# Second layer of a two-layer MoE kernel: the down product in seven products for eight per pair of token tiles, up products in blocks of 256 columns

## The chip, the cores and the metric

The kernel runs on one core of a Trainium2 chip. The metric is the device time of one execution in microseconds (us), taken as the median of several runs; lower is better. Durations come from one profiled execution of the kernel before, whose own time stands in the table below. PE is TensorE, DVE VectorE, ACT ScalarE, POOL GpSimd, SP SyncE.

## What is computed

A gated linear attention gives 3072 tokens of 384 columns. A router sends each to one of 8 experts, and a second, dense layer follows; its last three lines are the ones that matter here:

```python
h = np.maximum(x[mask] @ w1[e], 0.0)          # expert e, 384 -> 1024
out[mask] = gate_w[mask, None] * (h @ w2[e])  # 1024 -> 384
...
h = x @ w_in                                  # every token, 384 -> 2048
g = np.maximum(0.01 * h, h)
return (g @ w_out).astype(np.float32)         # 2048 -> 384
```

Every fp32 operand of a product is held as a pair of fp16 tiles, a high part and the rest (`hi`, `lo`), and every product is three matmuls: hi by hi, lo by hi, hi by lo.

## The kernel before

All is one function, `body`. Attention and routing come first and write each token with its gate into a DRAM table by expert (`bucket`) with indirect DMAs of POOL. Then the experts run one after the other with 432 places each, and in front of expert 0 stands a part of its tokens, 256 columns wide (`early=True`), that does not wait for the table. An expert's up product (L976 to L978) goes through four PSUM banks `ps1`; a bank is emptied by ACT (L983, the high part) and DVE (L984, the rest). Its down product (L1002 to L1004) ends in `x2h`/`x2l` (L1013, L1014), the second layer's input, 3072 columns in expert order. Beside it the next expert's weights and the second layer's weights are fetched by SP (L927), converted on ACT and DVE (L932, L933; L949 to L955) and split into pairs. The order of this stage is written by a planner (`Plan`): every step has an engine, a duration, what it reads and writes and a due time, and the planner's list sets the program order of every engine. Each engine works its list strictly from the top.

The second layer (functions `second_in` and `second_out`) takes 512 columns at a time, six blocks. `second_in` makes 16 hidden slices `f` of 128 rows, nine matmuls of 512 columns each (L809 to L811). For every slice ACT takes 0.01 times the sum (L814), DVE the larger of the two (L815), ACT the high part (L817), DVE the rest (L818). Then `second_out` takes the block's four tiles of 128 tokens one by one: 16 slices of three matmuls of 384 columns (L826 to L828), scaled by the gate on ACT (L830) and scattered to the output by POOL (L831). 24 tiles make 24 times 48 of these matmuls; the up part is 6 times 16 times 9 = 864 matmuls. Some 30 small DVE steps (`past_static`, L1073 to L1110) work out which tokens lie past an expert's 432 places; none do in this data, so the loop behind them runs no time.

Of the kernel before, what the change touches and what calls it, by code (L numbers as in the profile page):

```python
# [21 lines left out]
P = 128  # L22
# [138 lines left out]
OVB = 32  # L161
E0 = 2 * P
# [9 lines left out]
def body(ctx, tc, qT, kT, aT, v, emb, tau, w1, w2, w_in, w_out, out):  # L172
# [4 lines left out]
    wps = [ctx.enter_context(tc.tile_pool(name="wp0", bufs=1))]  # L177
# [29 lines left out]
    hid = [[keep.tile([P, BLK], F16, name=f"h{x}{f}") for f in range(NF1)] for x in "hl"]  # L207
# [3 lines left out]
    def stage():  # L211
        return wst.tile([P, CH], F32, name="wstage")
# [18 lines left out]
    def expert_tiles():  # L231
        wps.append(wps.pop(0))
        return [wps[-1].tile([P, KD * F1], F16, name=n) for n in ("w1h", "w1l", "w2h", "w2l")]
# [43 lines left out]
    with tc.tile_pool(name="at", bufs=1) as rt, \  # L277
# [394 lines left out]
        w_first = expert_tiles()  # L672
# [86 lines left out]
    wps.insert(0, ctx.enter_context(tc.tile_pool(name="wp1", bufs=1)))  # L759
    big = ctx.enter_context(tc.tile_pool(name="big", bufs=1))  # L760
    x2h = big.tile([P, KD, X2], F16, name="x2h")
    x2l = big.tile([P, KD, X2], F16, name="x2l")
# [3 lines left out]
    wol = big.tile([P, NF2, D], F16, name="wol")  # L766

# [35 lines left out]
    def second_in(gp, gs, pp, xh, xl, n):  # L803
        ghs, gls = [], []
        for f in range(NF2):
            ps = pp.tile([P, n], F32, name="ps3")
            fs = slice(f * P, (f + 1) * P)
            for k in range(KD):
                nc.tensor.matmul(ps, wih[:, k, fs], xh[:, k], start=k == 0, stop=False)  # L809
                nc.tensor.matmul(ps, wih[:, k, fs], xl[:, k], start=False, stop=False)  # L810
                nc.tensor.matmul(ps, wil[:, k, fs], xh[:, k], start=False, stop=k == KD - 1)  # L811
            r = gs.tile([P, n], F32, name="r")
            g = gs.tile([P, n], F32, name="g")
            nc.scalar.activation(r, ps, AF.Copy, scale=0.01 * 2.0 ** -6)  # L814
            nc.vector.scalar_tensor_tensor(g, ps, 2.0 ** -6, r, op0=ALU.mult, op1=ALU.max)  # L815
            gh, gl = (hid[i][f][:, :n] if f < NF1 else gp.tile([P, n], F16, name=f"g{i}{f}") for i in range(2))
            nc.scalar.activation(gh, g, AF.Copy)  # L817
            nc.vector.tensor_tensor(gl, g, gh, op=ALU.subtract)  # L818
            ghs.append(gh)
            gls.append(gl)  # L820
        return ghs, gls

    def second_out(gs, pp, ghs, gls, ts, scale, index, dst):
        ps = pp.tile([P, D], F32, name="ps4")
        for f in range(NF2):
            nc.tensor.matmul(ps, ghs[f][:, ts], woh[:, f], start=f == 0, stop=False)  # L826
            nc.tensor.matmul(ps, ghs[f][:, ts], wol[:, f], start=False, stop=False)  # L827
            nc.tensor.matmul(ps, gls[f][:, ts], woh[:, f], start=False, stop=f == NF2 - 1)  # L828
        osb = gs.tile([P, D], F32, name="osb")
        nc.scalar.activation(osb, ps, AF.Copy, scale=scale)  # L830
        nc.gpsimd.indirect_dma_start(out=dst, out_offset=bass.IndirectOffsetOnAxis(ap=index, axis=0),  # L831
                                     in_=osb, in_offset=None, bounds_check=NT - 1, oob_is_err=False)

    with tc.tile_pool(name="mx", bufs=1) as mxp, \
# [3 lines left out]
        first = [stage() for _ in range(4)]  # L838
        sets = [w_first, expert_tiles()]
# [155 lines left out]
        def down(e, d, at, cols, early=False):  # L995
# [16 lines left out]
            where = [] if e == 0 else [("place", i) for i in range(2)]  # L1012
# [4 lines left out]
        with tc.manual_schedule():  # L1017
# [23 lines left out]
            for e in range(E):  # L1041
# [13 lines left out]
                for d in range(KD):  # L1055
                    down(e, d, begin(e) + 13.2 + 4.4 * d - 12.0, cols)
            for i in plan.order():
                plan.ops[i][2]()
# [125 lines left out]
```

## Time and profile before

| | |
|---|---|
| runs of the kernel before | 773.33 to 776.7 us, median 773.78 us of 3 |
| the profiled execution | 771.36 us, its span 769.7 us |
| TensorE busy | 745.8 us, 97% of the span |
| VectorE busy | 453.6 us, 59% |
| ScalarE busy | 342.2 us, 44% |
| GpSimd busy | 97.7 us, 13% |

A matmul's duration in the trace holds its way through the array, and matmuls overlap; what one costs in a stream is the distance from its start to the next one's start. An engine's idle time costs only where another waits for it. All times in the rows are microseconds from the start of the span, unless marked ns.

### The profile page before, as it was taken

The numbers are of one execution on the slowest core, as the hardware profiler recorded it, in microseconds if no ns is written. First come the engines' busy times: TensorE is split into PE (matmuls) and PEld (weight loads), VectorE is DVE, ScalarE is ACT, GpSimd is POOL, SyncE is SP. The second block draws the span as 40 slices with busy tenths as digits, with TensorE's granted clock in tenths as the row PEclk, the third lists the DMA queues.
The fourth block names the chain that finished last, engine by engine and source line by source line (L and its number), as shares of the span: only waits on it lengthen the run. The fifth ranks groups of instructions, "written<-read, shape, count | busy, mean of one in ns | idle before, by whom it ended". The sixth has DMA issues, their size and how long they took to land.

```text
span 769.7 us, 13141 instructions
## 1 busy us (share of the span) xinstructions
PE 745.8 (97%) x5190; PEld 432.1 (56%) x5190; DVE 453.6 (59%) x795; ACT 342.2 (44%) x686; POOL 97.7 (13%) x108
## 2 busy tenths in 40 slices
PE   7999999989999999999899999999999999999995
PEld 4777767658655555555444654654554564564462
DVE  8989899958786898888955036016206305503600
ACT  2344545537665777776544035025215305403500
POOL 6121615140001000000000100110010010010011
PEclk9999999999999999999999999999999999999998
DMA  8994945248998999866200000000000000000000
GB/s 284 347 302 123 280 144 195 68 151 208 221 219 183 230 259 223 251 188 206 44 1 0 21 21 1 21 22 0 11 32 1 10 21 11 1 25 18 0 22 23
DMA packets 58754, 84.48 MB, mean 110 GB/s; under 512 B 26680, under 2 KB 37952, under 8 KB 58688
## 3 DMA queue, kind: packets, MB, share of 16 engines
q1 hardware_dynamic: 55072, 74.06, 35.6%
q0 software_dynamic: 3616, 9.53, 3.3%
q8 instruction: 43, 0.70, 0.4%
q14 instruction: 23, 0.19, 0.1%
HBM read 66.80 MB, written 12.12 MB: 103 GB/s over the span
## 4 chain that ended last, share of the span: by engine, by line
issue 47%; PE 34%; DVE 6%; DMA 5%; POOL 3%; ACT 2%; SPq 1%; POOLq 0%; ACTq 0%; DVEq 0%
PE ps L977 4%; PE ps L976 4%; PE ps L978 4%; PE ps L1004 3%; PE ps L1003 3%; PE ps L1002 3%; POOL out L831 3%; PE psc L403 3%; PE py L454 2%; PE py L422 2%; DMA wstage<-in_w_in 2%; PE pfill L343 2%; DMA v<-in_v 1%; DMA wstage<-in_w 1%; PE ptr L482 1%
## 5 line engine op out<-in xcount | busy, mean ns | idle before, releaser
L815 DVE SCALAR_TENSOR_TENSOR g<-ps,r 128x512 f32<-128x512 f32 x96 | 65.8, 685 | 154.9 <-ACT r L814 154.9
L809 PE MATMUL ps<-x2h,wih 128*128 128x512 f16 x288 | 109.9, 382 | 2.7 <-DVE x2l L1014 2.7
L810 PE MATMUL ps<-x2l,wih 128*128 128x512 f16 x288 | 109.9, 382 | 0.0
L811 PE MATMUL ps<-x2h,wil 128*128 128x512 f16 x288 | 109.7, 381 | 0.0
L830 ACT ACTIVATE osb<-ps,ms 128x384 f32<-128x384 f32 x24 | 13.9, 581 | 160.9 <-PE ps L828 160.9
L1004 PE MATMUL ps<-hh,w2l 128*128 128x432 f16 (+2 forms) x216 | 70.2, 326 | 0.3 <-DVE w2l L933 0.2
L1002 PE MATMUL ps<-hh,w2h 128*128 128x432 f16 (+2 forms) x216 | 70.2, 326 | 0.0
L1003 PE MATMUL ps<-hl,w2h 128*128 128x432 f16 (+2 forms) x216 | 70.2, 326 | 0.0
L831 POOL DMA_INDIRECT out<-osb,tki x24 | 23.3, 973 | 359.7 <-ACT osb L830 352.9
L976 PE MATMUL ps<-xt,w1h 128*128 128x432 f16 (+1 forms) x192 | 63.6, 333 | 0.9 <-ACT xt L901 0.9
L977 PE MATMUL ps<-xt,w1h 128*128 128x432 f16 (+1 forms) x192 | 63.6, 333 | 0.5 <-DVE xt L902 0.5
L978 PE MATMUL ps<-xt,w1l 128*128 128x432 f16 (+1 forms) x192 | 63.6, 333 | 0.1
L828 PE MATMUL ps<-woh,hl 128*128 128x384 f16 x192 | 62.6, 326 | 0.0
L826 PE MATMUL ps<-woh,hh 128*128 128x384 f16 x192 | 62.6, 326 | 0.0
L827 PE MATMUL ps<-wol,hh 128*128 128x384 f16 x192 | 62.6, 326 | 0.0
L828 PE MATMUL ps<-woh,g 128*128 128x384 f16 x192 | 62.6, 326 | 0.0
L827 PE MATMUL ps<-wol,g 128*128 128x384 f16 x192 | 62.6, 326 | 0.0
L826 PE MATMUL ps<-woh,g 128*128 128x384 f16 x192 | 62.6, 326 | 0.0
L814 ACT ACTIVATE r<-ps 128x512 f32<-128x512 f32 x96 | 56.0, 583 | 12.5 <-PE ps L811 12.5
L818 DVE TENSOR_TENSOR hl<-g,hh 128x512 f16<-128x512 f32 x48 | 33.3, 693 | 33.4 <-ACT hh L817 33.4
L818 DVE TENSOR_TENSOR g<-g,g 128x512 f16<-128x512 f32 x48 | 33.2, 693 | 33.4 <-ACT g L817 33.4
L810 PEld LDWEIGHTS <-wih 128*128 128x128 f16 x288 | 28.3, 98 | 36.8 <-issue 3.5
(226 smaller groups left out, 1347.0 us busy)
## 6 DMA issues: line engine op xcount, KB each, us to landing
wstage<-in_w SPq DMA_DIRECT2D x64, 384.0 KB, 5.5
a<-in_aT SPq DMA_DIRECT2D x16, 387.5 KB, 4.9
k<-in_kT SPq DMA_DIRECT2D x16, 384.0 KB, 5.9
q<-in_qT SPq DMA_DIRECT2D x16, 384.0 KB, 6.6
wstage<-in_w_in SPq DMA_DIRECT2D x16, 384.0 KB, 6.9
wstage<-in_w_out SPq DMA_DIRECT2D x16, 384.0 KB, 3.5
v<-in_v SPq DMA_DIRECT2D x8, 576.0 KB, 9.5
xg<-bucket SPq DMA_DIRECT2D x6, 582.0 KB, 6.9
```

Source lines behind the costliest of these rows:

```text
L809: nc.tensor.matmul(ps, wih[:, k, fs], xh[:, k], start=k == 0, stop=False)
L810: nc.tensor.matmul(ps, wih[:, k, fs], xl[:, k], start=False, stop=False)
L811: nc.tensor.matmul(ps, wil[:, k, fs], xh[:, k], start=False, stop=k == KD - 1)
L826: nc.tensor.matmul(ps, ghs[f][:, ts], woh[:, f], start=f == 0, stop=False)
L827: nc.tensor.matmul(ps, ghs[f][:, ts], wol[:, f], start=False, stop=False)
L828: nc.tensor.matmul(ps, gls[f][:, ts], woh[:, f], start=False, stop=f == NF2 - 1)
L976: nc.tensor.matmul(ps, w1h[:, f, k], xt[:, k], start=k == 0, stop=False)
L977: nc.tensor.matmul(ps, w1h[:, f, k], xt[:, KD + k], start=False, stop=False)
L978: nc.tensor.matmul(ps, w1l[:, f, k], xt[:, k], start=False, stop=k == KD - 1)
L1002: nc.tensor.matmul(ps, w2h[:, f, ds_], hh, start=f == 0, stop=False)
L1003: nc.tensor.matmul(ps, w2h[:, f, ds_], hl, start=False, stop=False)
L1004: nc.tensor.matmul(ps, w2l[:, f, ds_], hh, start=False, stop=f == NF1 - 1)
```

## The change

In the second layer the tokens go in 12 pairs of tiles (256 columns). `up` makes two hidden slices of a pair in one PSUM bank, 18 matmuls of 256 columns (five banks); `bent` applies the activation with ACT and DVE to both slices at once.

For the pairs 2 to 11 (`PLAIN = 2`) the down product is cut in halves three ways: by token tile, by hidden half (8 slices each) and by output half (192 columns). The eight partial products become seven: `operands` makes four sums of activation quarters on DVE (`s`) and splits all seven left operands into fp16 pairs, `combine` makes four sums of weight quarters once (T1 to T4, for each of 8 slices) and splits them, and `down` runs the seven products, each 8 slices of three matmuls of 192 columns. `taken` scales and adds each of the seven into the two tiles' outputs. The pairs 0 and 1 keep the plain down product (`plain_down`) while `combine` runs beside them; the sums of the weights go where expert 6 had its weights. The planner now sets the order of the second layer too; up products of the pairs ahead and down products stand in turn.

Since the seven products mix two tiles, `clear` writes zeros into `x2` past expert 0's places before expert 1 writes there: 12 ACT instructions of 660 fp32 elements, ordered by the planner in the expert stage. `x2` is now one tile per 128 rows and part (six tiles), the hidden tiles are one tile `held` whose memory also holds the activations later, the second layer's first up products take only rows 0 to 255 of `x2`, and the steps of `past_static` come during pair 4.

```diff
-    hid = [[keep.tile([P, BLK], F16, name=f"h{x}{f}") for f in range(NF1)] for x in "hl"]
+    held = keep.tile([P, 2, NF1, CAP], F16, name="held")
+    hid = [[held[:, i, f] for f in range(NF1)] for i in range(2)]
...
-    x2h = big.tile([P, KD, X2], F16, name="x2h")
-    x2l = big.tile([P, KD, X2], F16, name="x2l")
+    x2 = [[big.tile([P, X2], F16, name=f"x2{n}{d}") for d in range(KD)] for n in "hl"]
...
+    SEVEN = ((A11, B11), (S2, T2), (A12, B21), (S3, T3), (S1, T1), (A22, T4), (S4, B22))
...
+    def second_in(ps, xs, f0, ks):
+        n = xs[0][0].shape[-1]
+        for i in range(2):
+            fs = slice((f0 + i) * P, (f0 + i + 1) * P)
+            for k in ks[i]:
+                d = ps[:, i * n:(i + 1) * n]
+                nc.tensor.matmul(d, wih[:, k, fs], xs[0][k], start=k == 0, stop=False)
+                nc.tensor.matmul(d, wih[:, k, fs], xs[1][k], start=False, stop=False)
+                nc.tensor.matmul(d, wil[:, k, fs], xs[0][k], start=False, stop=k == KD - 1)
+
+    def bent(add, g, i, ps, key):
...
+        add("ACT", 0.59, lambda: nc.scalar.activation(dst, src, AF.Copy, scale=0.01), [key], [("g", i)])
+        add("DVE", 0.69, lambda: nc.vector.tensor_tensor(dst, src, dst, op=ALU.max), [key, ("g", i)], [("g", i)])
+
+    def operands(add, g, s, oh, ol, out):
+        lower, upper = ([g[:, i, h] for h in range(2)] for i in range(2))
+        sums = ((s[:, 0], lower[1], upper[1], ALU.add), (s[:, 1], s[:, 0], lower[0], ALU.subtract),
+                (s[:, 2], lower[0], lower[1], ALU.subtract), (s[:, 3], upper[0], s[:, 1], ALU.subtract))
...
+    def second_out(ps, o, j, k):
+        a, b = SEVEN[j]
+        oh, ol = (x[k // 2][:, a, k % 2] for x in o)
+        d = ps[:oh.shape[-1], :D2]
+        wh, wl = (out_weights(i, b, k) for i in range(2))
+        nc.tensor.matmul(d, oh, wh, start=k == 0, stop=False)
+        nc.tensor.matmul(d, oh, wl, start=False, stop=False)
+        nc.tensor.matmul(d, ol, wh, start=False, stop=k == NF1 - 1)
...
+            where = [[("place", i)] * (e > 0) + [("clear", i, d)] * (e == 1) for i in range(2)]
...
+        def clear(d, at):
+            w = (NT - CAP) // 4
+            for n in range(2):
+                for o in range(CAP, NT, 2 * w):
+                    x = x2[n][d][:, o:o + 2 * w].bitcast(F32)
+                    plan.add(S_, 0.16 + w / 1200, lambda x=x: nc.scalar.activation(x, row0[:, 0:1].to_broadcast([P, w]), AF.Copy), [], [("clear", n, d)], at=at)
...
+        def combine(k):
...
+            for i in range(2):
+                add(V, 0.56, lambda i=i: nc.vector.tensor_tensor(w[:, i * D:(i + 1) * D], woh[:, i * NF1 + k], wol[:, i * NF1 + k], op=ALU.add), [], own[2 * i:2 * i + 2])
...
+            for dst, x, y in ((q[T1], b12, b11), (q[T3], b22, b12), (q[T2], b22, q[T1]), (q[T4], b21, q[T2])):
+                add(V, 0.36, lambda dst=dst, x=x, y=y: nc.vector.tensor_tensor(dst, x, y, op=ALU.subtract), own, ["quarters"])
...
+            for b in range(5):
+                up(0, b, ((0, 1), ()))
+            for b in range(5):
+                up(0, b, ((2,), range(KD)))
...
+                    if g < 2 and j % 2 and g * 4 + j // 2 < NF1:
+                        combine(g * 4 + j // 2)
+                    (plain_down if g < PLAIN else down)(g, j)
```

Three places show how the program order moves. The first is ACT's list where expert 0's early part begins (line numbers of the changed kernel are larger: L1043 is L983 before, L1083 is `clear`, L1050 is L990). Before:

```order
L983 ACTIVATE hh_98<-ps_1925 128x256 [waits DVE_49,PE_49,Activation_49]
L983 ACTIVATE hh_99<-ps_1926 128x256 [waits PE_49]
L983 ACTIVATE hh_100<-ps_1927 128x256 [waits PE_49]
L983 ACTIVATE hh_101<-ps_1928 128x256 [waits PE_49]
L983 ACTIVATE hh_102<-ps_1925 128x256 [waits PE_49]
```

and with the change, in the same place:

```order
L1083 ACTIVATE x2h_1870<-row_86 128x660 [waits DMASW4_49,DMASW3_49,DMASW5_49,DMASW2_49,DMASW6_49,DMASW1_49,DMASW7_49,DMASW0_49,DMAHW5_49,DVE_49,DMAHW6_49,PE_49,DMAHW7_49,Activation_49,Pool_49]
L1083 ACTIVATE x2l_1873<-row_86 128x660
L1043 ACTIVATE held<-ps_1911 128x256 [waits PE_49,Activation_49]
L1083 ACTIVATE x2h_1870<-row_86 128x660
L1043 ACTIVATE held<-ps_1912 128x256 [waits PE_49]
L1083 ACTIVATE x2l_1873<-row_86 128x660
L1043 ACTIVATE held<-ps_1913 128x256 [waits PE_49]
```

Two clears stand ahead of the first emptying of a `ps1` bank, and the first of them waits for all queues of POOL's DMAs (DMASW), among which are the last six scatters into `bucket`: `x2` lies where the attention's tiles lay.

The second is DVE's list at the seam between the layers, up to the last step of `x2l`. Before (L1092 to L1103 are `past_static`):

```order
L955 SCALAR_TENSOR_TENSOR wol<-t_1924,woh 128x384
L1094 TENSOR_TENSOR shared<-shared,c_4194 128x288
L1098 TENSOR_TENSOR ee_4215<-ee_4215,o_4210 128x288
L1095 TENSOR_REDUCE o_4210<-shared 128x32
L1099 COPY o_4210<-ee_4215 128x32
L1103 TENSOR_TENSOR o_4210<-shared,o_4210 128x32
L1100 TENSOR_TENSOR ee_4215<-ee_4215,c_4194 128x288
L1014 ISA
L1014 SCALAR_TENSOR_TENSOR x2l<-ps_1932,x2h 128x432
```

and with the change (L1216 to L1222 are `combine`, L1074 is L1014 before):

```order
L1015 SCALAR_TENSOR_TENSOR wol<-t_1910,woh 128x384
L1219 TENSOR_TENSOR shared<-wstage,shared 128x192 x2
L1216 TENSOR_TENSOR wstage<-woh,wol 128x384 x2
L1222 TENSOR_TENSOR w2h<-shared,w1h 128x768
L1074 ISA
L1074 SCALAR_TENSOR_TENSOR x2l_1875<-ps_1918,x2h_1872 128x432
```

`past_static` is gone from there, and the sums of the first two weight slices stand ahead of the last `x2l`.

The third is DVE's list inside the second layer. Before it is one pair of rows, again and again:

```order
L815 SCALAR_TENSOR_TENSOR g_4241<-ps3_4230,r_4240 128x512
L818 TENSOR_TENSOR hl0_106<-g_4241,hh0_98 128x512
L815 SCALAR_TENSOR_TENSOR g_4257<-ps3_4246,r_4256 128x512
L818 TENSOR_TENSOR hl1_107<-g_4257,hh1_99 128x512
L815 SCALAR_TENSOR_TENSOR g_4273<-ps3_4262,r_4272 128x512
```

and with the change, for four hidden slices of a pair (L831 is `bent`, L847 the four sums, L843 the split into fp16, L870 `taken`):

```order
L843 SCALAR_TENSOR_TENSOR o1l2_4205<-held_98,o1h2_4201 128x256
L831 TENSOR_TENSOR held_98<-u0_4182,held_98 128x2x2x128
L847 TENSOR_TENSOR st_4190<-held_98 128x256
L847 TENSOR_TENSOR st_4190<-st_4190,held_98 128x256
L847 TENSOR_TENSOR st_4190<-held_98 128x256
L847 TENSOR_TENSOR st_4190<-held_98,st_4190 128x256
L843 SCALAR_TENSOR_TENSOR o1l2_4205<-held_98,o1h2_4201 128x512
L870 SCALAR_TENSOR_TENSOR wstage_1880<-c2_4189,ms_4180,wstage_1882 128x192
L843 SCALAR_TENSOR_TENSOR o1l2_4205<-st_4190,o1h2_4201 128x1024
L831 TENSOR_TENSOR held_98<-u1_4183,held_98 128x2x2x128
```

DVE has four sums, a wider split and the adding of products between two activations, where it had two steps a slice.

## Rows read from the trace of the kernel before

**Rows 1.** The page of the kernel before: span, and busy time by engine.

```profile
span 769.7 us, 13141 instructions
PE 745.8 (97%) x5190; PEld 432.1 (56%) x5190; DVE 453.6 (59%) x795; ACT 342.2 (44%) x686; POOL 97.7 (13%) x108
```

**Rows 2.** Busy time by stretch: stretch and its length, then each engine, TensorE clock, DMA.

```profile
186.05:381.91 195.86, 195.48 (x1151) 109.24 (x1151) 164.46 (x306) 134.61 (x257) 10.79 (x17) 1.00 0.85 206
381.91:760.29 378.38, 375.69 (x2017) 197.61 (x2015) 128.87 (x209) 122.35 (x216) 22.38 (x23) 1.00 0.04 13
```

**Rows 3.** Timeline, TensorE, second layer: start us, duration us, engine, line, out<-in.

```profile
388.39 0.38 PE L809 MATMUL ps<-x2h,wih 128*128 128x512 f16 x1
399.61 0.38 PE L810 MATMUL ps<-x2l,wih 128*128 128x512 f16 x1
...
749.72 0.33 PE L828 MATMUL ps<-woh,g 128*128 128x384 f16 x1
759.96 0.33 PE L828 MATMUL ps<-woh,g 128*128 128x384 f16 x1
```

**Rows 4.** Timeline, TensorE, expert 0: products of 256 and of 176 columns.

```profile
175.64 0.27 PE L978 MATMUL ps<-shared,w1l 128*128 128x256 f16 x1
183.50 0.27 PE L1004 MATMUL ps<-hh,w2l 128*128 128x256 f16 x1
...
193.27 0.24 PE L1003 MATMUL ps<-hl,w2h 128*128 128x176 f16 x1
196.98 0.24 PE L1004 MATMUL ps<-hh,w2l 128*128 128x176 f16 x1
```

**Rows 5.** One line of the kernel, its weight loads: count, ns min/median/max, first and last start.

```profile
L1002 PEld LDWEIGHTS <-w2h x216: 96/98/98, 175.6 to 381.2; 128*128 128x128 f16 x108
```

**Rows 6.** Timeline, the seam between the layers; in brackets idle time and what ended it.

```profile
381.73 0.35 PE L1004 MATMUL ps<-hh,w2l 128*128 128x432 f16 x1
384.10 0.60 DVE L1014 SCALAR_TENSOR_TENSOR x2l<-ps,x2h 128x432 f32 x1
384.76 0.59 PE L809 MATMUL ps<-x2h,wih 128*128 128x512 f16 x1 [2.69 <-DVE x2l L1014]
```

**Rows 7.** Timeline, expert 0: ScalarE, TensorE and the queue of SyncE (SPq).

```profile
168.67 0.38 ACT L983 ACTIVATE hh<-ps 128x256 f16<-128x256 f32 x1 [3.89 <-PE ps L978]
171.82 0.27 PE L976 MATMUL ps<-shared,w1h 128*128 128x256 f16 x1
173.58 0.33 SPq L927 DMA_DIRECT2D wstage<-in_w_in  x1
...
184.14 0.49 ACT L901 ACTIVATE xt<-ps 128x384 f16<-128x384 f32 x1
185.03 0.28 ACT L901 ACTIVATE xt<-ps 128x144 f16<-128x144 f32 x1
```

**Rows 8.** Groups by line and shape: busy us, mean ns of one, idle before.

```profile
L815 DVE SCALAR_TENSOR_TENSOR g<-ps,r 128x512 f32<-128x512 f32 x96 | 65.8, 685 | 154.9 <-ACT r L814 154.9
L953 DVE TENSOR_TENSOR t<-t,shared 128x384 f32<-128x384 f32 x32 | 17.7, 554 | 2.5 <-ACT t L952 1.7
L933 DVE SCALAR_TENSOR_TENSOR w1l<-wstage,w1h 128x768 f16<-128x768 f32 x28 | 26.5, 952 | 3.2 <-ACT w1h L932 2.9
L984 DVE SCALAR_TENSOR_TENSOR hl<-ps,hh 128x256 f16<-128x256 f32 x8 | 3.3, 424 | 4.5 <-ACT hh L983 4.5
L1076 DVE TENSOR_TENSOR ob<-ob,n_e 128x192 f32<-128x192 f32 x1 | 0.4, 358 | 0.1
L932 ACT ACTIVATE w1h<-wstage 128x768 f16<-128x768 f32 x28 | 23.1, 832 | 3.1 <-DMA wstage<-in_w 2.9
L983 ACT ACTIVATE hh<-ps 128x256 f16<-128x256 f32 x8 | 3.0, 381 | 7.6 <-PE ps L978 7.6
```

**Rows 9.** Waits of the second layer: who for whom, us in total, times, longest.

```profile
DVE hl L818 <- ACT hh L817: 33.4, 48, 0.7
```

**Rows 10.** Timeline, the end of the program, ScalarE.

```profile
760.37 0.58 ACT L830 ACTIVATE osb<-ps,ms 128x384 f32<-128x384 f32 x1 [7.27 <-PE ps L828]
```

More of the change, by code (lines that the diff above doesn't have):

```diff
@@ L801, in expert_out @@
         return ps
[L803 to L830, printed above, removed]
+    B11, B21, B22 = ((0, 0), (NF1, 0), (NF1, 1))
@@ new lines, in product, with keyed, go, own @@
+        def product(us, fn, reads, writes):
+            add(T_, us, fn, reads, writes, after=["pe"] if "pe" in plan.wrote else ())
+            plan.wrote["pe"] = len(plan.ops) - 1
+        def keyed(n, slot):
+            def go(eng, us, fn, reads, writes):
+                def own(k):
+                    return k + (slot,) if k[0] == "g" else k
+                add(eng, us, fn, [own(k) for k in reads], [own(k) for k in writes])
+            return go
+        done = 0
+        def up(g, b, ks=ALL):
+            kk, i = divmod(b, 2)
+            bank, slot = (g * UP + b) % 5, (g * UP // 2 + kk) % 3
+            xs = [[x[:, g * PAIR:(g + 1) * PAIR] for x in x2[n]] for n in range(2)]
+            product(sum(len(k) for k in ks) * 0.3275, lambda: second_in(banks[bank], xs, NF1 * i + 2 * kk, ks), [], [("b", bank)] if 0 in ks[0] else [("ub", bank)])
+            if not ks[1]:
+                return
+            to = keyed(g, slot)
+            bent(lambda eng, us, fn, r, w: to(eng, us, fn, r + [("ub", bank)], w), gs[slot], i, banks[bank], ("b", bank))
+            if i:
+                o = ops16[g % 2][0][kk], ops16[g % 2][1][kk], ("o", g % 2, kk)
+                operands(to, gs[slot], st, *o) if g >= PLAIN else plain_operands(to, gs[slot], *o)
@@ new lines, in down @@
+        def down(g, j):
+            a, c = SEVEN[j][0], (2 * PLAIN + 7 * (g - PLAIN) + j) % 3
+            part = 0 if a == A11 else 1 if a <= A22 else 2
+            for kk in range(NF1 // 2):
+                product(0.495, lambda kk=kk: [second_out(sums[c], ops16[g % 2], j, k) for k in (2 * kk, 2 * kk + 1)],
+                        [("o", g % 2, kk, part, i) for i in range(2)] + [("tq", k, i) for k in (2 * kk, 2 * kk + 1) for i in range(2)], [("c", c)])
+            taken(add, j, c, sums[c], us[g % 2], osbs[g % 2], [ms[:, 2 * g + h, 0:1] for h in range(2)], g % 2, g % 2)
+            if j in (5, 6):
+                deliver(g, 6 - j)
```

245 lines of the change are left out of this document (182 added, 63 removed).

## The prediction, made before the changed kernel ran

> **What bounds the kernel now.** I read the page first: of a span of 769.7 us TensorE is busy 745.8, 97%, and no other engine is over 59% [rows 1]. A share over the whole span hides stages, so the table by stretch came next. From 186.05 to 381.91 us, the experts, TensorE is busy 195.48 of 195.86; from the last expert matmul to the end of the second layer 375.69 of 378.38 [rows 2]. In both the reader should see a full TensorE at clock 1.00, and DVE in the second layer at 128.87 of 378.38, a third. So the second layer costs the sum of its matmuls' spacings, and the change has to be priced in matmuls; then come the places where TensorE could newly wait. For spacings I took starts in the timeline, since a listed duration holds the way through the array: 52 matmuls of 512 columns between 388.39 and 399.61 are 0.2158 each, 63 of 384 columns between 749.72 and 759.96 are 0.1625 [rows 3]; 72 of 256 columns are 0.1092, 49 of 176 columns 0.0757 [rows 4].
>
> The only idle stretch is the seam: the last expert matmul starts at 381.73 and ends its part at about 381.91, the next starts at 384.76, behind the last step of x2l on DVE [rows 6]. The nine matmuls that start from 384.76 on end at 388.39 [rows 3, 6]; at 0.2158 they would take 1.94, and they took 3.63, near twice that: the lower of the two clock levels (1.2 instead of 2.4 GHz) after the idle time.
>
> **The change part by part**, against the profiled execution's own 771.36 us. The median of the runs is 2.42 higher.
>
> 1. *Up products.* 864 of 512 columns become 1728 of 256: 1728 x 0.1092 = 188.7 for 864 x 0.2158 = 186.4. **+2.2**.
>
> 2. *Down products.* Two pairs of twelve stay: 192 matmuls of 384 columns. The other ten had 960 x 0.1625 = 156.0 and get 1680 of 192 columns. No row has 192 columns. The nearest, 176, went at 0.0757, and the line from there to 256 gives 0.0757 + 16 x 0.00042 = 0.0824. Bounds: 0.0757 below; above, 0.098, what one weight load takes [rows 5], if loads paced the stream. I take 0.0824, since the 176 columns ran beside the same loads. 1680 x 0.0824 = 138.4. **-17.6**. (With 0.098: +8.6.)
>
> 3. *Seam.* The first 30 matmuls now read only rows 0 to 255 of x2, finished before; 30 x 0.1092 = 3.3 us of work lies over the wait. The 2.85 us of gap and the 3.63 - 1.94 = 1.69 of low clock go: **-4.5**. Late next is the second part of the loop, which wants the last x2l at about 382.0 + 3.3 = 385.3. That step, 0.60 on DVE [rows 6], is rid of past_static but has two weight slices' sums and a split ahead of it, and the matching ACT split too; I put it at 385.4. **+0.3** (0 to 1.5).
>
> 4. *DVE and the handovers.* The steps, by rows of equal size [rows 8]: an activation of 512 from PSUM 0.685, a sum of 256 at most 0.424, splits of 256, 512 and 1024 elements 0.424, 0.69 and (extended from 512 and 768) 1.22, a product of 192 columns taken 0.358. A pair with seven products: 8 x 0.685 + 16 x 0.42 + 4 x 2.33 + 8 x 0.36 = 24.4 us. TensorE's pair: 144 x 0.1092 + 168 x 0.0824 = 29.6. DVE is at 83%, from 34%. In a plain pair DVE has 16 steps of 0.685 (11.0) and four weight slices at 2 x 0.554 + 4 x 0.358 + 0.952 = 3.49, 25.0 against 15.7 + 96 x 0.1625 = 31.3. Until the first seven-product begins, TensorE has 27 blocks of 18 up products at 1.97 and 31.2 of plain products, 84.3 us, and DVE some 76 us of work, 91%. past_static's 30 small steps, at most 30 x 0.36 = 10.7, go into pair 4's slack of 5.2 a pair, with five banks and three slots of activations to lend time. So nearly all hides; **+1.0** for a wait here and there (0 to +10; DVE waiting for ACT within a slice is the row that says waits exist: 48 times, 0.7 each [rows 9]). The upper end is ten pairs at 1 us.
>
> 5. *Clears.* ACT's list has two clears ahead of the first emptying of a ps1 bank, which ran at 168.67 [rows 7]. The first clear waits for the last scatters of the table. So does SyncE's load at 173.58 [rows 7], whose wait names the same six scatters: they landed at about 173.55. ACT is in order, so the emptying waits too. A clear of 660 elements is between 0.381 (256) and 0.832 (768) [rows 8], about 0.74; two end at 175.05, the emptying at 175.4, DVE's part 0.42 later, 175.9. TensorE has four banks; its fifth product, at 171.82 [rows 7], now waits till then: +4.1. After such a wait I expect the low clock again, priced by the seam's 1.69: +1.7. The second eviction of xt, at 185.03 behind one ending at 184.63 [rows 7], is likely to close up: -0.4. Behind it nothing absorbs the loss: from 186.05 on TensorE is full [rows 2], and weights, gathers and tables shift along. **+5.4** (0 to 6.5). The other ten clears, 7.4 us of ACT, fall where ACT is at 134.61 of 195.86 [rows 2]: nothing.
>
> 6. *End.* The last step is DVE's 0.36 instead of ACT's 0.58 [rows 8, 10]: **-0.2**.
>
> Sum: 2.2 - 17.6 - 4.5 + 0.3 + 1.0 + 5.4 - 0.2 = **-13.4**, 758.0 for the profiled execution, **760.4** on the median's scale.
>
> **The rivals** (all on the median's scale; 0.5% is about what a measurement of this kernel can tell from no change, so 769.9 and 777.6 are the borders).
>
> *Early clears cost nothing.* If the scatters land sooner than I read it, or the first banks are emptied elsewhere, the 5.4 go: 755.0. For it: the landing is inferred from one load's start. Against: that load's list names the same scatters, and ACT's order is fixed.
>
> *DVE late.* Seven products want all their operands before the bank turns; DVE's chain for a pair (activation, sums, split) waits for ACT's halves several times. Each such wait could cost 0.7 as in [rows 9]. Eight a pair that nothing fills make 24.4 into 30.0, over TensorE's 29.6; the point is about 5.2 us of waits a pair. In ten pairs that gives 3 to 12 us, 764 to 772, centre 767. For: 91% up to the first seven-product, and operands that come in three parts. Against: DVE works strictly from a list in which other slices' steps stand between such pairs, and three slots of activations are in hand. It makes a slowdown only from 31 us of DVE per pair upward.
>
> *Weight loads pace the short products (slower).* Place: the 1680 products of 192 columns. If each takes as long as one weight load, 0.098 [rows 5], that is 1680 x 0.0156 = 26.2 more: **786.6**. The forecast's gain ends at a spacing of 0.0904 (13.4 / 1680 above 0.0824), and it is slower by over 0.5% from 0.0927. Against: 176 columns went at 0.0757 while their loads are listed at 0.098 [rows 4, 5], so loads overlap one another too; each product here also brings a new stationary tile, as there. For: only 49 such matmuls were seen in a row, and the seven products run 168 a pair.
>
> The Trainium skill, page "TensorE: Matmul & The Clock Gate", section "LDWEIGHTS (loading the stationary operand)", prices a load at columns divided by 1.2, in ns, and its section "Back-to-back issue gap" says that in a stream the spacing is set by both operations. As an estimate from that page, 128 columns are 0.107 us, and if loads of that length paced the products the sum would be 41 us higher, about 802. The trace agrees with the load's length (0.098) but not with its pacing: 0.0757 for 176 columns is below it.
>
> That the program does not do fewer columns is no rival: the counts of products are in its text, and 1680 x 192 is seven eighths of 960 x 384.
>
> **How the numbers follow.** Forecast, with its own bounds (756 to 764): 0.60. Clears free (755): 0.13. DVE late (764 to 772): 0.19, three quarters of it below 769.9. Weight loads (786.6): 0.05. The remaining 0.03 are mishaps of both signs. The range 753.5 to 769.0 takes in the first two and most of the third, and leaves out weight loads and DVE's tail; the ends of step 2 (0.0757 gives 11 us less) stay out, since the slope between two rows is firm. Faster by over 0.5%: 0.60 + 0.13 + 0.14 + 0.01 = 0.88. Within: 0.05. Slower: 0.05 + 0.02 = 0.07.
>
> **What would show it.** Right: starts of the 192-column products 0.082 apart and of the 256-column ones 0.109; no idle time of TensorE at the seam and clock 1.00 behind it; DVE at 80 to 85% from pair 2 on, with TensorE's idle time there under 2 us in all; one wait of about 4 us at 172, ended by ACT's emptying of ps1 behind the clears, with a lower clock after it; the stretch from there to the last expert matmul as long as before. Wrong: short products at 0.09 or more (weight loads); TensorE waiting for operands at every pair, or for a bank that DVE has not read (DVE late); clears that begin before 173 (clears free); a seam that moves its wait to the 31st product; or a longer expert stretch, since then the other clears, or the transfers that they shift, cost too.

## The result, and the profile after

The changed kernel took 763.07 us (median of 4, 762.43 to 764.68), the kernel before beside it 775.0: a ratio of 0.985, 95% interval 0.982 to 0.988, 11.9 us. Twice more, on other occasions, it was 761.93 against 769.91 (0.991, 0.988 to 0.993) and 759.74 against 769.43 (0.986, 0.984 to 0.988): 8.0 and 9.7 us. Forecast were 13.4 us and 760.4. The profiled execution of the changed kernel took 762.96.

The page after, answering to [rows 1]:

```profile
span 761.3 us, 16644 instructions
PE 729.9 (96%) x6774; PEld 561.6 (74%) x6774; DVE 601.3 (79%) x1131; ACT 388.4 (51%) x746; POOL 99.8 (13%) x108
```

TensorE lost 15.9 us of work, DVE went from 59% to 79%. The table by stretch of the changed kernel (stretch and length, then busy time of PE, PEld, DVE, ACT, POOL, then clock, DMA), cut at the first early product, the first 176-column product, the end of the experts, the first product of the second layer and the last:

```profile
170.11:194.51 24.40, 18.45 (x150) 15.61 (x151) 12.31 (x31) 14.73 (x31) 4.87 (x6) 0.86 0.48 154
194.51:390.77 196.26, 195.19 (x1152) 109.58 (x1152) 165.20 (x299) 136.54 (x263) 9.16 (x14) 1.00 0.81 205
390.77:393.07 2.30, 0.17 (x1) 0.00 (x0) 2.22 (x4) 1.16 (x2) 0.00 (x0) 1.00 0.41 6
393.07:751.75 358.68, 358.61 (x3600) 326.38 (x3599) 273.82 (x550) 161.85 (x263) 25.83 (x26) 1.00 0.04 14
```

The last row answers to the second of [rows 2]: TensorE is busy for 358.61 of 358.68 us with DVE at 273.82. No wait is left in the second layer once it has begun. What idles now lies ahead: 5.95 us in the first row, and 2.1 at the seam.

The first and the last 192-column product of a run at the end, 84 in all, start 6.85 us apart, 6.85 / 83 = 0.0825 each, and the weight loads of this line (count, ns min/median/max) are as long as in [rows 5]:

```profile
744.81 0.25 PE L857 MATMUL c<-w1l,o1h 128*128 128x192 f16 x1
751.66 0.25 PE L859 MATMUL c<-woh,o1l 128*128 128x192 f16 x1
```

```profile
L857 PEld LDWEIGHTS <-o1h x280: 96/98/98, 506.8 to 751.4; 128*128 128x128 f16 x140
```

The forecast had 0.0824. The early part of expert 0, answering to [rows 7]:

```profile
170.11 0.27 PE L1036 MATMUL ps<-shared,w1h 128*128 128x256 f16 x1 [0.41 <-DVE ohs L757]
177.46 0.33 SPq L987 DMA_DIRECT2D wstage<-in_w_in  x1
177.53 0.75 ACT L1083 ACTIVATE x2h<-row 128x660 f32<-128x660 f32 x1 [8.87 <-DMA bucket<-xb,slot]
178.19 0.73 ACT L1083 ACTIVATE x2l<-row 128x660 f32<-128x660 f32 x1
178.83 0.36 ACT L1043 ACTIVATE held<-ps 128x256 f16<-128x256 f32 x1
179.22 0.42 DVE L1044 SCALAR_TENSOR_TENSOR held<-ps,held 128x256 f16<-128x256 f32 x1 [7.58 <-ACT held L1043]
179.70 0.37 PE L1036 MATMUL ps<-shared,w1h 128*128 128x256 f16 x1 [5.51 <-DVE held L1044]
180.08 0.42 PE L1038 MATMUL ps<-shared,w1l 128*128 128x256 f16 x1
183.44 0.27 PE L1036 MATMUL ps<-shared,w1h 128*128 128x256 f16 x1
```

Here the reader sees step 5 happen: SyncE's load and the first clear begin together at 177.5, when the last scatter has landed; a second clear follows; then the emptying of the first bank at 178.83, DVE's half at 179.22, and TensorE's fifth product at 179.70 after 5.51 us. From there to 183.44 the products stand 0.21 apart: the low clock level. The kernel before has such a stretch too, only earlier, among its first products. The granted clock (0.50 is 1.2 GHz, 1.00 is 2.4 GHz) stands behind the busy times, first for the kernel before, then for the changed one:

```profile
166.34:169.75 3.41, 3.41 (x18) 2.35 (x17) 1.65 (x8) 0.38 (x1) 2.50 (x4) 0.50 0.39 141
176.53:183.36 6.83, 3.66 (x18) 2.61 (x18) 2.03 (x5) 5.32 (x11) 0.70 (x1) 0.50 0.22 61
```

So the kernel before began its fifth product (of nine matmuls each) 5.59 us after the first (166.23 to 171.82, [rows 7]). In a second profile of it (e9 below), with the clock at 1.00 there, it began 3.92 us after the first:

```profile
170.03 0.27 PE L976 MATMUL ps<-shared,w1h 128*128 128x256 f16 x1
```

The seam, answering to [rows 6]:

```profile
390.59 0.35 PE L1064 MATMUL ps<-held,w2l 128*128 128x432 f16 x1
390.66 0.84 ACT L1221 ACTIVATE w1h<-shared 128x768 f16<-128x768 f32 x1 [1.40 <-DVE shared L1219]
391.54 0.96 DVE L1222 TENSOR_TENSOR w2h<-shared,w1h 128x768 f16<-128x768 f32 x1
392.41 0.60 DVE L1074 SCALAR_TENSOR_TENSOR x2l<-ps,x2h 128x432 f32 x1
393.07 0.27 PE L823 MATMUL u<-x2h,wih 128*128 128x256 f16 x1 [2.13 <-DVE x2l L1074]
```

The first product of the second layer still waits for the last x2l on DVE, in front of which stands combine's split (391.54). It reads rows 0 to 255, which were finished long before. The clock stayed at 1.00 behind this gap.

To compare executions I cut each trace at the same places (lengths in us from starts in the timeline):

| execution | start to first early product | early part | experts | gap | second layer |
|---|---|---|---|---|---|
| before | 166.23 | 19.13 | 196.55 | 2.85 | 375.20 |
| before, again (e9) | 166.11 | 18.24 | 197.09 | 2.86 | 373.52 |
| changed | 170.11 | 24.40 | 196.26 | 2.30 | 358.59 |
| changed, again (e1) | 166.42 | 24.34 | 197.99 | 2.31 | 360.25 |
| changed, again (e10) | 169.63 | 22.64 | 196.42 | 2.32 | 360.25 |
| clears late (e2) | 165.85 | 19.67 | 196.28 | 1.43 | 358.36 |
| banks by name (e3) | 166.06 | 25.44 | 198.56 | 0.00 | 358.35 |
| both (e4) | 168.70 | 19.08 | 198.68 | 0.00 | 358.36 |
| both, again (e11) | 167.66 | 18.82 | 197.41 | 0.00 | 358.36 |
| whole order (e5) | 171.14 | 24.41 | 196.26 | 1.43 | 358.36 |
| all plain (e6) | 172.62 | 24.29 | 196.26 | 1.54 | 375.67 |
| two DVE sums more (e7) | 174.27 | 22.74 | 196.25 | 2.30 | 359.31 |
| five DVE sums more (e8) | 174.14 | 22.75 | 196.26 | 2.30 | 383.09 |
| both, whole order (e12) | 167.88 | 17.88 | 197.14 | 0.00 | 359.02 |

The gain is all in the last two columns, 17.2 us between the first two profiles and 13.8 between e9 and e10, and about a third of it is given back in the early part. The first column lies ahead of the parts that were changed, and it differs by up to 8.4 us. The five executions above 170 us have a late start of ScalarE there (last section), and several have stretches at the low clock (granted 0.50 from 13.41 to 20.24 us in e10).

### The profile page after: what moved, and what is told of

It reads as the page before. It is cut to its first block, busy times and chain, and to the rows that moved or that the text cites. A ratio compares the mean times of both kernels' runs of the same rounds, so it can differ in the third digit from the quotient of the medians.

```text
span 761.3 us, 16644 instructions
## 1 busy us (share of the span) xinstructions
PE 729.9 (96%) x6774; PEld 561.6 (74%) x6774; DVE 601.3 (79%) x1131; ACT 388.4 (51%) x746; POOL 99.8 (13%) x108
## 4 chain that ended last, share of the span: by engine, by line
PE 84%; DVE 7%; DMA 3%; ACT 2%; issue 1%; POOL 1%; another core or an unknown queue 1%; SPq 0%; ACTq 0%; POOLq 0%; DVEq 0%
PE u L823 8%; PE u L824 8%; PE u L825 8%; PE c L857 6%; PE c L859 6%; PE c L858 6%; PE ps L1036 4%; PE ps L1037 4%; PE ps L1038 4%; PE ps L1063 4%; PE ps L1064 4%; PE ps L1062 4%; PE psc L407 3%; DMA v<-in_v 2%; PE py L426 2%; PE py L458 2%
## 5 line engine op out<-in xcount | busy, mean ns | idle before, releaser
L823 PE MATMUL u<-x2h,wih 128*128 128x256 f16 x576 | 157.0, 273 | 2.1 <-DVE x2l L1074 2.1
L824 PE MATMUL u<-x2l,wih 128*128 128x256 f16 x576 | 157.0, 273 | 0.0
L825 PE MATMUL u<-x2h,wil 128*128 128x256 f16 x576 | 157.0, 273 | 0.0
L831 DVE TENSOR_TENSOR held<-u,held 128x512 f32<-128x512 f32 x96 | 65.9, 687 | 56.0 <-ACT held L830 55.9
L830 ACT ACTIVATE held<-u 128x512 f32<-128x512 f32 x96 | 57.3, 597 | 86.5 <-PE u L825 83.1
L1063 PE MATMUL ps<-held,w2h 128*128 128x432 f16 (+2 forms) x216 | 70.2, 326 | 0.3 <-DVE held L1044 0.3
L1062 PE MATMUL ps<-held,w2h 128*128 128x432 f16 (+2 forms) x216 | 70.2, 326 | 0.0
L1064 PE MATMUL ps<-held,w2l 128*128 128x432 f16 (+2 forms) x216 | 70.2, 326 | 0.0
L824 PEld LDWEIGHTS <-wih 128*128 128x128 f16 x576 | 56.4, 98 | 9.1 <-issue 2.4
L823 PEld LDWEIGHTS <-wih 128*128 128x128 f16 x576 | 56.4, 98 | 6.8
L825 PEld LDWEIGHTS <-wil 128*128 128x128 f16 x576 | 56.4, 98 | 6.5
L1043 ACT ACTIVATE held<-ps 128x432 f16<-128x432 f32 (+2 forms) x72 | 34.9, 487 | 20.7 <-PE ps L1038 20.4
L870 DVE SCALAR_TENSOR_TENSOR wstage<-c,ms,wstage 128x192 f32<-128x192 f32 x80 | 31.8, 411 | 16.9 <-PE c L859 16.8
L347 PE MATMUL pfill<-busy,ones 128*128 128x512 f16 x121 | 39.9, 403 | 2.1 <-POOL busy L194 2.1
## 6 DMA issues: line engine op xcount, KB each, us to landing
k<-in_kT SPq DMA_DIRECT2D x16, 384.0 KB, 10.6
```

What stands on the lines that cost most here:

```text
L823: nc.tensor.matmul(d, wih[:, k, fs], xs[0][k], start=k == 0, stop=False)
L824: nc.tensor.matmul(d, wih[:, k, fs], xs[1][k], start=False, stop=False)
L825: nc.tensor.matmul(d, wil[:, k, fs], xs[0][k], start=False, stop=k == KD - 1)
L830: add("ACT", 0.59, lambda: nc.scalar.activation(dst, src, AF.Copy, scale=0.01), [key], [("g", i)])
L831: add("DVE", 0.69, lambda: nc.vector.tensor_tensor(dst, src, dst, op=ALU.max), [key, ("g", i)], [("g", i)])
L1062: nc.tensor.matmul(ps, w2h[:, f, ds_], hh, start=f == 0, stop=False)
```

## The experiments

**The changed kernel again (e1).** No edit; the first profile held what looked like an accident, a late start of ScalarE on `yT` in the attention, that had to be told from the change.

> The changed kernel once more. Its first profile has something that neither the change nor the prediction speaks of: in the attention's last part ScalarE starts the eviction of yT (L469) at 158.61 us, about 3.2 us after the product that it waits for, where the kernel before starts it at once (155.74). Theory A: that is an accident of one execution; then this profile has no such wait (ScalarE's idle time before the last L469 about 2 us, not 5.1), the first early up product starts near 166 us, not 170.1, and the execution's own time is 3 to 4 us under the first profile's 762.96. Rival: it belongs to the changed program (its list of instructions is longer); then it is there again, at the same place and size. Both expect the wait of 4 to 5.5 us of the fifth early up product behind the clears, and 2.1 us at the seam.

761.93 us. The accident is not there (L469 starts after 1.93 us of idle time, as before), the first early product starts at 166.42, the wait behind the clears is 5.55 and the gap 2.31. But the execution was hardly shorter, against what theory A expected: 1.7 us went into waits in the experts, nearly all for `held` on DVE, and 1.7 into the start of the second layer, where this time the low clock followed. Its timeline there:

```profile
391.06 0.34 PE L823 MATMUL u<-x2h,wih 128*128 128x256 f16 x1 [2.14 <-DVE x2l L1074]
391.20 0.42 PE L824 MATMUL u<-x2l,wih 128*128 128x256 f16 x1
391.41 0.42 PE L825 MATMUL u<-x2h,wil 128*128 128x256 f16 x1
...
394.69 0.27 PE L823 MATMUL u<-x2h,wih 128*128 128x256 f16 x1
```

Steps of 0.21 from 391.20 on, where the first profile has 0.11 behind a gap of the same length.

**Clears late (e2).**

```diff
-  ... nc.scalar.activation(x, row0..., AF.Copy), [], [("clear", n, d)], at=at)
+  ... nc.scalar.activation(x, row0..., AF.Copy), [("x2", 0, d)], [("clear", n, d)], at=at)
```

> The changed kernel with one edit: each of the twelve clears waits in the planner for expert 0's own last x2 step of its part, so that none stands among the early evictions on ScalarE. Theory: the early clears cost what step 5 says, the wait of TensorE (5.5 us in the first profile) and the low clock after it (17 matmuls at 0.21 instead of 0.109, 1.8 us), less what closes up: 5 us, so 4.5 to 6 us under the changed kernel in the same job, and the wait of PE ps L1036 on DVE held L1044 gone from the list. Rival: the early products would wait anyway for the scatters by another way (their tiles lie where the attention's lay, or the next weights come late); then the wait only changes its releaser and the time moves by less than 1.5 us.

755.36 us, 6.6 under e1 and a little over the 6 that were expected at most (ratio to before 0.981, 0.979 to 0.983). The early part fell from 24.34 to 19.67, 4.7 us. The two profiled executions lie 9.7 us apart: e1's waits in the experts (1.7) and its low clock behind the seam (1.9) are absent here, the gap is 0.9 shorter, and 0.6 lies ahead of the early part. How much of these the other runs share is not shown. TensorE's wait on DVE held is gone; the timeline has the emptying at once, the fifth product without an idle time, and SyncE's load still at the scatters' landing:

```profile
168.30 0.38 ACT L1043 ACTIVATE held<-ps 128x256 f16<-128x256 f32 x1 [3.89 <-DVE offi L760]
171.44 0.27 PE L1036 MATMUL ps<-shared,w1h 128*128 128x256 f16 x1
173.33 0.33 SPq L987 DMA_DIRECT2D wstage<-in_w_in  x1
```

So the scatters do not hold the products back by another way, and the twelve clears, now between 195 and 213 us, cost nothing there: the experts take 196.28, as before.

**Banks by name (e3).**

```diff
+    turn = ExitStack()
+    pm = turn.enter_context(tc.tile_pool(name="pm", bufs=1, space=PSUM))
+    ps1 = [pm.tile([P, 512], F32, name=f"ps1{i}") for i in range(4)]
+    ps2 = [pm.tile([P, 512], F32, name=f"ps2{i}") for i in range(4)]
...
-            tc.tile_pool(name="pn", bufs=1, space=PSUM) as pn:
...
-        banks = [pn.tile([P, 2 * PAIR], F32, name=f"u{i}") for i in range(5)]
-        sums = [pn.tile([P, 512], F32, name=f"c{i}") for i in range(3)]
+        banks = [*ps1, ps2[0]]
+        sums = ps2[1:]
```

> The changed kernel with one edit: the second layer uses the eight PSUM banks of the expert stage by name (u0 to u3 are ps1, u4 and c0 to c2 are ps2) instead of a new pool. Nothing else moves. Theory: the 2.1 us wait of the first second-layer product is the hand-over of the whole pool, which asks for the last x2l step (on a row range that these products don't read); with banks by name the first 30 products start at once behind the last expert product, 3.3 us of work over a wait of 2.1: 2.1 us under the changed kernel (1.5 to 2.6, with nothing for the clock, which stayed at 1.00). Rival: the products really need that x2l step, or a bank is still read; then the wait stays or goes to a later product of the thirty and the time moves by less than 0.7 us.

760.13 us, 1.8 under e1. The timeline of the seam:

```profile
389.88 0.35 PE L1065 MATMUL ps<-held,w2l 128*128 128x432 f16 x1
390.06 0.27 PE L823 MATMUL ps<-x2h,wih 128*128 128x256 f16 x1
390.70 0.52 ACT L1074 ACTIVATE x2h<-ps 128x432 f32 x1
```

The first product starts 0.18 us behind the last expert product, while the last x2h is still to come on ScalarE at 390.70. The gap was the hand-over of the pool of PSUM banks, not data. The time itself says little alone (755.79 to 762.35 in six runs); the rows show it.

**Both edits (e4).**

> Both edits, clears late and banks by name. Theory: the two waits lie one behind the other in a stream that is full between them, so the gains add: 6.5 to 8.5 us under the changed kernel in the same job, and TensorE has no wait over 1 us from the first early up product to the end. Rival: the time won early is lost later, since weights and gathers then come late for the experts; then the gain is that of the banks alone, and new waits on DMA or on w1/w2 splits appear in the expert stage.

753.04 us, 8.9 under e1, a little more than expected, and 0.977 of the kernel before (0.976 to 0.979). Early part 19.08, gap 0.00, second layer 358.36. TensorE had one early wait of 1.4 us, for xs on DVE, so not all waits are under 1 us. The experts took 198.68 in this execution against 196.28 in e2. More than half of the difference is the clock:

```profile
187.98:191.40 3.42, 2.96 (x22) 2.92 (x21) 2.92 (x7) 2.27 (x7) 0.83 (x1) 0.50 1.28 314
```

The granted clock was 0.50 there, and from 187.68 to 191.09 in e11, whose experts took 197.41; in e2 such a stretch lay among the early products instead. Waits on DVE at 299 us, for `w2l` above all, under 0.9 us together, are what is left for the rival's late weights. The 198.56 of e3 has another cause: its clock stayed at 1.00 through the experts, and TensorE waited 1.2 and 0.8 us at 264 and 270 us for ScalarE and DVE.

**Whole order at the seam (e5).**

```diff
-            for b in range(5):
                 up(0, b, ((2,), range(KD)))
```

(the line then stands in the first loop).

> The changed kernel with one edit: the first five up blocks of the second layer run whole, one after the other, without the order that takes rows 0 to 255 of x2 first. Theory: since the very first product waits for the last x2l step (the pool's hand-over), the split order covers nothing in the changed kernel, and this one has the same gap of 1.3 to 2.3 us at the seam and the same time as the changed kernel (761.9 in the job before) within 1 us. Rival, step 3 of the prediction: the split order does cover a wait; then the gap grows, and the time by 2 us or more.

763.61 us, beside a kernel before at 776.02 (0.984, 0.980 to 0.987): 12.4 under it, where the changed kernel itself was 8.0 to 11.9 under its own. The changed kernel did not run in this comparison, so "the same time" is not shown more closely. The second layer took 358.36, and its first product still waits for the last x2l: in the changed kernel the split order covers nothing. The gap is 1.43, where the changed kernel has 2.30, since combine's split, too, fell behind x2l in this order:

```profile
392.58 0.61 DVE L1074 SCALAR_TENSOR_TENSOR x2l<-ps,x2h 128x432 f32 x1 [0.50 <-ACT x2h L1073]
```

DVE is idle here until x2h is there. So of the 2.30 us some 0.9 is combine's split in front of x2l, and 1.4 is the hand-over with x2h and x2l themselves.

**All pairs plain (e6).**

```diff
-PLAIN = 2
+PLAIN = 12
...
-                    if g < 2 and j % 2 and g * 4 + j // 2 < NF1:
-                        combine(g * 4 + j // 2)
```

> The changed kernel with PLAIN = 12 and without combine: every pair keeps the plain down product, all the rest of the change stays (256-column up products, clears, new order, pairs). Theory: the seven products are worth step 2, 960 x 0.1625 - 1680 x 0.0824 = 17.6 us, and nothing else of them shows; so this takes 17 to 18.5 us more than the changed kernel (about 779.5), which is slower than the kernel before by 8 to 11 us. Rival: the activations in pairs, sums and takings cost TensorE waits of their own in the changed kernel; then less than 16 us come back.

780.63 us, 17.0 over e5 of the same comparison and slower than the kernel before (1.006, 1.003 to 1.008). The table by stretch has 2880 products without a gap, DVE at a third of the time:

```profile
394.71:770.70 375.99, 375.99 (x2880) 281.68 (x2879) 136.53 (x223) 129.13 (x215) 22.71 (x24) 1.00 0.04 13
```

The second layer took 375.67 instead of 358.36: the seven products are worth 17.3 us where step 2 says 17.6, and bring no waits of their own.

**More work on DVE (e7, e8).** Two extra sums a step in e7, five in e8, of which nothing is read.

```diff
+                for _ in range(2 if g >= PLAIN else 0):
+                    to("DVE", 0.42, lambda: nc.vector.tensor_tensor(sx, gs[slot][:, 0, 1], gs[slot][:, 1, 1], op=ALU.add), ...)
```

> The changed kernel with two more DVE sums of 256 columns (0.42 us each, into a tile that nobody reads) for each two-slice step of the pairs 2 to 11: 8 x 0.42 = 3.4 us more DVE work a pair, 33.6 in all. It adds work and takes none away. Theory (step 4): DVE has 29.6 - 24.4 = 5.2 us of slack a pair, so this costs nothing to 3 us. Rival (DVE late): DVE's chain with ScalarE has no real slack, and what is added shows at a good part: 10 us or more.

> The same with five sums a step: 20 x 0.42 = 8.4 us more a pair, over the slack. Theory: DVE paces the pairs 2 to 11 at 24.4 + 8.4 = 32.8 us (and its own pipeline gaps), 3.2 us over TensorE's 29.6, in ten pairs 32 us more, 28 to 45; TensorE's waits on DVE appear in these pairs only. Rival (DVE late): about 8.4 us a pair show, 70 to 84 us.

e7: 766.85 us, 3.2 over e5; in the second layer 0.7 to 0.95 us (359.31), the rest ahead of it, where nothing was edited: the granted clock was 0.50 from 159.13 to 172.79 in this execution, from 160.53 to 163.94 in e5's, and the gap is 0.9 longer than e5's. e8: 790.44, 26.8 over e5, and 24.7 in the second layer, a little under the 28 that were expected. TensorE's waits in the second layer, first e7, then e8 (us in total, times, longest; e8 has the wait for x2l as well):

```profile
PE u L823 <- DVE x2l L1074: 2.1, 1, 2.1
PE c L857 <- DVE wstage L870: 0.8, 1, 0.8
```

```profile
PE c L857 <- DVE wstage L870: 18.0, 10, 5.6
```

And e8's busy time in two stretches (columns as above), DVE at 75.69 and 76.68 of 80, TensorE now below it in the first:

```profile
520.00:600.00 80.00, 73.17 (x741) 68.03 (x739) 75.69 (x180) 30.97 (x50) 4.21 (x4) 0.96 0.03 11
600.00:680.00 80.00, 76.85 (x804) 71.76 (x802) 76.68 (x168) 34.81 (x59) 6.31 (x6) 1.00 0.05 16
```

3.4 us more a pair cost 0.1, 8.4 us more cost 2.5: the slack is some 5.9 us a pair, where step 4 says 5.2. Up to 4 of e8's 24.7 us are the clock, granted at 0.50 from 562.01 to 568.83 and from 756.57 to 759.98, around its longest waits; without them the slack would come to 6.3. In the changed kernel DVE is close to a bound but not one.

**Before and after on one chip (e9 to e12).**

> The kernel before, as an entry of its own, so that its profile stands beside the changed kernel's from the same chip. ScalarE's late start of the last yT (L469, 3.2 us) was in the first profile of the changed kernel, in none of the four of the second job and in all four of the third. Theory A2: it goes with the chip of a job, not with the program; then in this job either the kernel before (its line is L465) and the changed kernel both show it (5.1 to 5.2 us of idle time, releaser not in this trace) or neither does. Rival: it comes from the changed program; then the changed kernel can show it here and the kernel before does not.

769.32 us. No late yT in it, and none in e10. That fits a cause that goes with the chip, and does not prove it: e9 to e12 ran on the chip of e1 to e4, which had shown none, and e5 to e8 on another. Its seam is the more telling part:

```profile
383.65 0.60 DVE L1014 SCALAR_TENSOR_TENSOR x2l<-ps,x2h 128x432 f32 x1
384.30 0.38 PE L809 MATMUL ps<-x2h,wih 128*128 128x512 f16 x1 [2.70 <-DVE x2l L1014]
384.52 0.38 PE L810 MATMUL ps<-x2l,wih 128*128 128x512 f16 x1
384.73 0.38 PE L811 MATMUL ps<-x2h,wil 128*128 128x512 f16 x1
```

The same gap as in [rows 6], 2.70 us, and behind it steps of 0.215, the full clock, where the first profile of the kernel before had the low one.

> The changed kernel beside the kernel before and the two that follow, on one chip. Theory: 8 to 13 us under the kernel before, as in the comparisons so far (11.9, 8.0); by the stages of the trace 17 us less in the second layer and its seam, 5 us more in the early part of expert 0. Rival: none; this is the base of the other three.

759.74 us, 9.7 under the kernel before. The second layer took 13.3 us less (with the low clock at this seam, 360.25), the gap 0.5 less, 13.8 together where 17 were expected; the early part 4.4 more for 5. Its wait behind the clears is shorter than the first profile's:

```profile
PE ps L1036 <- DVE held L1044: 3.8, 1, 3.8
```

Of the 36 matmuls of the four up products ahead of that wait those from the ninth on, 170.56 to 173.8 us, stood 0.21 apart here, at the low clock, and so filled more of the time to the scatters' landing. Behind the wait the clock was at 1.00.

> Clears late and banks by name once more, on this chip. Theory: 7 to 9.5 us under the changed kernel of this job (8.9 in the second job), no wait of TensorE at the seam, early part of expert 0 about 19 us long as in the kernel before instead of 24.4. Rival: what the second job showed was that chip's; then less than 5 us.

753.55 us, 6.2 under e10 (0.978 of before, 0.976 to 0.981): less than the 7 expected, with the edits' own stages as expected (early part 18.82, gap 0.00).

> Both edits, and the first five up blocks in whole order, without the split that takes rows 0 to 255 of x2 first. Theory: with the banks by name the seventh product is the first to want the last x2l step, 0.66 us after the first; of a wait of 1.4 to 2.1 us then 0.8 to 1.5 come back, at the seventh product, and the time is 0.8 to 3 us over e11 (the upper end with the lower clock after it). Rival: the split is worth nothing even then, because the last x2l step ends early enough: same time and no wait.

753.23 us, no more than e11. In the trace of the whole order the wait is there, and small:

```profile
382.90 0.27 PE L823 MATMUL ps<-x2h,wih 128*128 128x256 f16 x1
383.67 0.61 DVE L1075 SCALAR_TENSOR_TENSOR x2l<-ps,x2h 128x432 f32 x1 [2.29 <-ACT x2h L1074]
383.69 0.27 PE L823 MATMUL ps<-x2h,wih 128*128 128x256 f16 x1
384.33 0.27 PE L824 MATMUL ps<-x2l,wih 128*128 128x256 f16 x1 [0.38 <-DVE x2l L1075]
```

With both edits combine's split no longer holds up the last x2h and x2l, in e11 either: x2l begins 0.77 us after the first product in both, for 1.64 in e3. TensorE waits 0.38 us for it, and 0.66 us is lost in the second layer (359.02 for 358.36). The expected 0.8 to 3 us do not show in the time. With banks by name the split is worth some 0.7 us by the trace.

## Why the prediction was right or wrong

The direction and the forecast's range held. The gain was smaller, 8.0 to 11.9 us for 13.4. By its steps:

1. and 2. *Products: right.* Steps 1 and 2 and the plain pairs give 188.7 + 31.2 + 138.4 = 358.3 us; the stages without low clock took 358.4 to 358.6. Against 373.52 (e9, full clock) that is 15.0 less, for 2.2 - 17.6 = -15.4.

3. *Seam: wrong, and the largest miss.* The step that failed is that "the first 30 matmuls now read only rows 0 to 255 of x2, finished before; 30 x 0.1092 = 3.3 us of work lies over the wait", for -4.5 with +0.3 behind it. What the products read is true, and not what they wait for: the second layer's banks come from a new pool that takes the place of the old, and its first product waits until the last reader of the old pool is done. Of 2.85 us, about 0.5 went, in every profile of the changed kernel. e3 shows the cause: without the turn of the pool, gap zero. The +0.3 for a late x2l would not have been needed: in e3 the last x2l ends 2.24 us behind the first product (390.06 to 392.30), inside the 3.3 us.
The other part of step 3, 1.69 us of low clock, was priced as a fixed cost from one profile. The runs make it a toss: after gaps of 2.1 to 2.7 us the low level followed in three profiles (before, e1, e10) and not in two more of the same two programs (e9, the changed kernel's first), nor in e7 and e8, so it is neither saved nor lost by this change with certainty.

4. *DVE: right in kind.* By the traced groups (columns: busy, mean ns)

```profile
L831 DVE TENSOR_TENSOR held<-u,held 128x512 f32<-128x512 f32 x96 | 65.9, 687 | 56.0 <-ACT held L830 55.9
L870 DVE SCALAR_TENSOR_TENSOR wstage<-c,ms,wstage 128x192 f32<-128x192 f32 x80 | 31.8, 411 | 16.9 <-PE c L859 16.8
L843 DVE SCALAR_TENSOR_TENSOR o0l<-st,o0h 128x1024 f16<-128x1024 f32 x20 | 24.5, 1225 | 2.2 <-ACT o0h L842 2.2
```

a pair costs 8 x 0.687 + 16 x 0.42 + 8 x 0.411 + 4 x 2.33 = 24.8 us, for 24.4; the taking of a product is dearer than the 0.358 of step 4. In the middle of the stage DVE is at 75 to 79%, under the 80 to 85% that the prediction named as its sign:

```profile
520.00:600.00 80.00, 80.00 (x846) 75.59 (x845) 60.28 (x116) 36.27 (x60) 6.35 (x6) 1.00 0.05 16
600.00:680.00 80.00, 80.00 (x851) 75.75 (x850) 62.80 (x122) 36.73 (x59) 4.64 (x5) 1.00 0.03 11
```

The sum of durations, 24.8, would be 84% of 29.6. It is too much because DVE's listed durations overlap where one step follows another: at the seam the split begins at 391.54 and is listed with 0.96, and x2l begins at 392.41, before that has run out. So DVE has a little more room than step 4 says, as e7 and e8 found. The +1.0 for waits was not spent. The rival "DVE late" falls by the missing wait in the table by stretch.

5. *Clears: the sum right, in part by luck.* Forecast +5.4: 4.1 for the fifth product's delay, 1.7 of low clock behind it, 0.4 closed up. Against the profile it was priced from, this is what came: the fifth product began 4.0 us later after the first (9.59 for 5.59), the low clock behind it cost 1.8, and 0.5 closed up. But the wait is 5.5 us and not 4.1. The start of the fifth product that the step used, 171.82, already held 1.7 us of low clock, which it took for a stream at full clock; in e9 that clock is not there. Nor is the 1.7 behind the wait a price of the clears: every one of the fourteen profiles, e2 and e9 among them, has one stretch at 0.50 somewhere between the first early product and 192 us. The two slips nearly cancel. With the experts' column added, so that this stretch lies inside in every profile, the clears and what hangs on them cost 5.0 us (first profiles) and 3.7 (e10 against e9), and e2 took 4.7 back in the early part. The landing that was inferred from one load's start is the one the clear waits for: the first clear began 7.4 us after the first early product, and 7.3 was forecast. So "early clears cost nothing" falls too.

6. The end is 0.1 us shorter, for 0.2.

The sum with the measured terms: -15.0 - 0.5 + 3.7 to 5.0 - 0.1 is -10.6 to -11.9, with the clock at the seam 1.7 either way, and what differs ahead of the change (the first early product starts at 165.9 to 174.3 in these executions) on top. The medians are -8.0, -9.7 and -11.9. Step 3 promised 4.2 and the gap gave 0.5: these 3.7 us are the largest part of what the 13.4 had too much. The +1.0 of step 4 that was not needed, and up to 1.7 of step 5, made up for some of it.

The rival "weight loads pace the short products" falls by 0.0825 us a product under loads of 0.098. The Trainium skill, page "TensorE: Matmul & The Clock Gate", section "Back-to-back issue gap", gives columns divided by 2.4 plus 2.5, in ns, as the gap of a single product and says that at small sizes it is too low, because weight loads are not in it. For 192 columns that is an estimate of 0.0825; here, in a stream with a load for each product, the trace agrees with the formula and shows no addition at 192 columns.

## What to carry to other kernels

A tile's data need not be all that its first use waits for: where a stage opened new PSUM banks over old ones, as here, its first instruction waited for the last reader of the old ones, whatever it read itself. A cheap instruction that waits costs what stands behind it in an in-order list: two clears of 0.74 us ahead of the first emptying cost 4 to 5 us here, and nothing where e2 has them, from 195 us on. A start that a price is read from has a clock of its own: 1.7 us of the fifth product's start was low clock. When a saturated engine's work is cut, its spacing times count is a price to trust (358.3 forecast, 358.4 to 358.6 measured), while what the clock does after a short gap should go into the range, not into the sum. The version with both waits removed (e4, e11) is 753.0 to 753.6 us, 16 to 17 under the kernel before and 6 to 9 under the change.

## What the runs showed of the hardware that had not been expected

The low clock level after an idle time of 2 to 3 us comes in some executions of one program and not in others, as told in step 3. In the early part of expert 0, too, it moves: in the kernel before it began at 166.34 in one profile and at 184.97 in the other, behind the same idle times of 1.44 and 0.41 us ahead of the first early product.

ScalarE began the last yT of the attention 3.2 us late in the first profile of the changed kernel, and as late in all four of e5 to e8, always with 5.1 to 5.2 us of idle time, but in none of the other profiles, with the edits' programs on either side. The changed kernel's row (e5's has 5.22):

```profile
158.61 0.71 ACT L469 ACTIVATE yT<-py 112x384 f32<-112x384 f32 x2 [5.09 <-remote]
```

The releaser is not in the trace, the product that it waits for was done (1.93 us of idle time elsewhere). The kernel before took 776.0 us beside e5 to e8 and 775.0 in the first comparison, against 769.4 and 769.9 in the two comparisons without it, so it seems to belong to a chip or its condition rather than to the change; the kernel before was not profiled beside a late yT, and the cause stays open.
